# Second norms in a skewed order: the next pair's passes between a pair's root and its remainders, squares summed to a variance, remainders spread, 14 idle products for 24

## The chip, the cores and the metric

The kernel is one program on one core of one Trainium2 chip. The metric is the device time in microseconds of one execution, lower is better. Five engines run side by side, each through its own queue in order: PE (TensorE, matrix products; its weight loads are listed as PEld), DVE (VectorE), ACT (ScalarE), POOL (GpSimd), and SP (SyncE), which here only issues DMAs.

## The reference

Input is a sequence of 2048 rows of 640 channels, in fp32. Two blocks, each behind a layer norm with a modulation and a gated residual, are applied one after the other:

```python
mod = (_silu(c) @ w_mod).reshape(c.shape[0], 6, 1, -1)
sa, ca, ga, sb, cb, gb = (mod[:, 0], mod[:, 1], mod[:, 2], mod[:, 3], mod[:, 4], mod[:, 5])
h = _layernorm(x, axis=-1) * (1 + ca) + sa
x = x + ga * _A_ref(h, A_k, A_v, A_shift_k, A_ssm_k, A_ssm_D)
h = _layernorm(x, axis=-1) * (1 + cb) + sb
x = x + gb * _B_ref(h, B_w1, B_b1, B_w2, B_b2)
```

`_A_ref` is a short convolution, a product, a long convolution over the sequence and a gate. `_B_ref` is a token mixer: **a second layer norm of h**, then `u = gelu(h^T w1 + b1)` with 1728 hidden units, then `u w2 + b2`. So between block A and block B each row of x goes through two norms in a row: the first over x, with the modulation `(1 + cb)`, `sb`, and the second over its result. The change concerns that place alone.

## The kernel before

Rows and channels: the 2048 rows stand as 16 groups j of 128 rows (one row per partition), 640 channels each, in `xa` (j 0 to 7) and `xb` (j 8 to 15). Two groups make a pair; the pairs are 0 to 7.

The first 270 us or so compute block A, channel block by channel block. Its last part, `i1` and `gate` for the last channel block, finishes x. Then comes the stage of the two norms, whose results feed the first product of block B, x h against w1. The hidden units stand in 14 blocks f. The first four are accumulated side by side while the norms still run: `products(pr)` adds the two groups of a pair to the four blocks f 0 to 3, each held in a PSUM tile (`acc`). The later blocks (f from 4) take all 16 groups at a time, one block after the other, and need no more of the norms. After them come the products with w2.

fp32 accuracy is had by splitting: every operand is a rounded "half" (fp32r) and a "rest", the difference. A product is half x half, half x rest, rest x half; so one pair costs 2 groups x 4 blocks x 3 kinds x 2 column halves = 48 matmuls of 128x320.

For a pair pr the steps of the stage are:

- `x1_stats`: on DVE, the mean and variance of two groups of x (`bn_stats` for the last channel block, `bn_aggr`, lines 548 and 717).
- `root_in(n)` and `root(n)`: 1/sqrt(variance + eps). `roots` (line 721) lists which second norms and which first norms share one root, since a root is a few short instructions whose cost hardly depends on how many values it holds. Before, POOL adds eps, and turns the sum of squares into a variance (lines 737 and 740); ACT takes the square root (line 741); DVE takes the reciprocal and one Newton step (lines 326 to 329), and the first norm's shift (line 750).
- `norm1(pr)`: on ACT, (x - mean)/sigma into x itself or, for j < 4, into other memory (line 755).
- `second(pr)`: on DVE, two passes over each group: times `(1 + cb)` with a running sum (line 761), then less the mean and plus `sb` (line 766). Then on ACT the sum of squares (line 771).
- `halves(pr)`: on ACT, the row scaled by its second root, rounded (line 775). `rests(pr)`: on DVE, the difference (line 779).
- `products(pr)`: on PE (line 445).

Beside the norms, the rows of w1 for blocks 0 to 3 have to be split too: `split_rows(r, ...)` takes the fourth r of the groups, ACT makes the halves (line 420), DVE the remainders (line 422, listed under the helper's line 57). `load_rows` brings r = 2 and 3 into `x` and `p`; when `x` has been read, `load_w(4)` loads the weights of block 4 into it. After the stage `split_w(4)` splits block 4 (lines 434 and 436) and `u_evac(f, ...)` takes the first four blocks out of PSUM through gelu, freeing PSUM tiles in the order f = 0, 1, 2, 3; block 4 is accumulated in the tile that f = 0 leaves.

The order of everything is the order in which the code issues it (a manual schedule): each engine works through its own instructions in that order and waits at the head of its queue. The idle products of line 817 (results overwritten) stand on PE ahead of `products(0)`.

Of the kernel before, what the change touches and what calls it, by code (L numbers as in the profile page):

```python
# [47 lines left out]
def mixer_kernel(ctx: ExitStack, tc: tile.TileContext, q, k, v, shift_k, ssm_k, ssm_D, w1, b1, w2, b2, c,  # L48
# [7 lines left out]
    act, dve, pool, pe, sync = nc.scalar, nc.vector, nc.gpsimd, nc.tensor, nc.sync  # L56
# [3 lines left out]
    def mem(tag, n, name=None):  # L60

        return sb.tile([128, n], F32, name=name or tag, tag=tag, bufs=1)
# [261 lines left out]
    def newton(r, t, v, n=None):  # L324

        dve.reciprocal(r, t)
        dve.scalar_tensor_tensor(t, r, -0.5, r, op0=ALU.mult, op1=ALU.mult)
        TT(dve, t, t, v, ALU.mult)
        dve.scalar_tensor_tensor(r, t, 1.5, r, op0=ALU.add, op1=ALU.mult)
# [384 lines left out]
    def x1_stats(js):  # L714
        for j in js:
            x1s(NC - 1, j)()
            dve.bn_aggr(mv[:, j, :], bst[:, j])


    V_, T_, R_ = (T_kt[:, o:o + 32] for o in (1280, 1312, 1344))  # L720
    place = {}
    roots = (((), (0, 1)), ((0, 1), (2, 3)), ((2, 3), (4, 5)), ((4, 5), (6, 7, 8, 9)), ((6, 7), (10, 11)),
             ((8, 9), (12, 13)), ((10, 11), (14, 15)), ((12, 13), ()), ((14, 15), ()))
    start = []
    for second_, first_ in roots:
# [5 lines left out]

    def root_in(n):

        second_, first_ = roots[n]
        o = start[n]
        if second_:
            pool.tensor_scalar(V_[:, o:o + 2], V_[:, o:o + 2], 1 / D, EPS, op0=ALU.mult, op1=ALU.add)
            o += 2
        if first_:
            pool.tensor_scalar(V_[:, o:start[n + 1]], mv[:, first_[0]:first_[-1] + 1, 1], EPS, None, op0=ALU.add)  # L740
        act.activation(T_[:, start[n]:start[n + 1]], V_[:, start[n]:start[n + 1]], AF.Sqrt)

    def root(n):

        o = slice(start[n], start[n + 1])
        newton(R_[:, o], T_[:, o], V_[:, o])
        first_ = roots[n][1]
        if first_:
            f = slice(first_[0], first_[-1] + 1)
            dve.scalar_tensor_tensor(nm1[:, f], mv[:, f, 0], -1.0, R_[:, start[n + 1] - len(first_):start[n + 1]],  # L750
                                     op0=ALU.mult, op1=ALU.mult)

    def norm1(pr):
        for j in (2 * pr, 2 * pr + 1):
            act.activation(row(j), XR(j), AF.Identity, scale=at(R_, 1, j), bias=nm1[:, j:j + 1])

    def second(pr):

        for j in (2 * pr, 2 * pr + 1):
            t = row(j)  # L760
            dve.scalar_tensor_tensor(t, t, 1.0, CB, op0=ALU.mult, op1=ALU.mult, accum_out=su[:, j:j + 1])
        n = su[:, 2 * pr:2 * pr + 2]
        dve.tensor_scalar(n, n, msb, -1 / D, op0=ALU.add, op1=ALU.mult)
        for j in (2 * pr, 2 * pr + 1):
            t = row(j)
            dve.scalar_tensor_tensor(t, t, su[:, j:j + 1], SB, op0=ALU.add, op1=ALU.add)
        for j in (2 * pr, 2 * pr + 1):
            if j == 12:
                H.extend(unit(mem("xa", 5120, "h_x"), 4))
            H[j] = H[j][:, 0:640], H[j][:, 640:1280]  # L770
            act.activation(H[j][1].bitcast(F32R), row(j), AF.Square, accum_out=at(V_, 2, j))

    def halves(pr):
        for j in (2 * pr, 2 * pr + 1):
            act.activation(H[j][0].bitcast(F32R), row(j), AF.Identity, scale=at(R_, 2, j))

    def rests(pr):
        for j in (2 * pr, 2 * pr + 1):
            dve.scalar_tensor_tensor(H[j][1].bitcast(F32R), row(j), at(R_, 2, j), H[j][0], op0=ALU.mult,
                                     op1=ALU.subtract)  # L780
# [32 lines left out]
    for r, t in ((2, X), (3, P)):  # L813
        load_rows(r, t)
    acc.append(psum().rearrange("p (h m) -> p h m", h=2))
    for i in range(24):
        pe.matmul(acc[0][:, i % 2, 0:320], blk[0][0][:, 0].bitcast(F32R),
                  blk[1][0].rearrange("p j m -> p (j m)")[:, 0:320].bitcast(F32R), start=True, stop=True)
    second(0)
# [43 lines left out]
    products(7)  # L863

    U = {}
    thirds = lambda t, n, o=0: [t[:, o + 320 * i:o + 320 * i + 320] for i in range(n)]
# [323 lines left out]
```

## Time and profile before

| what | value |
|---|---|
| times of three runs | 675.30, 676.17, 678.89 us; median 676.17 us |
| profiled execution: first to last instruction (span) | 673.9 us |
| its mean granted TensorE clock | 0.979 |
| busy PE / DVE / ACT / POOL | 628.9 / 497.5 / 300.1 / 133.5 us |
| the same inside 268 to 356 us | 79.3 / 70.5 / 52.9 / 5.4 us |

The profiled execution has no time of its own beside its span in what is shown; the median of the runs is 2.27 us above that span, the fastest run 1.4 us. In the timeline a row is: start, length, engine, line, operation, output and inputs, shapes, count, and in brackets how long the engine had been idle and what ended that. Starts are in microseconds from the start of the span. A row's length includes the pipeline's tail, so that consecutive rows overlap a little: what an instruction costs its engine is the distance to the next start.

### The profile page before, as it was taken

The numbers are of one execution on the slowest core, as the hardware profiler recorded it, in microseconds if no ns is written. First come the engines' busy times: TensorE is split into PE (matmuls) and PEld (weight loads), VectorE is DVE, ScalarE is ACT, GpSimd is POOL, SyncE is SP. The second block draws the span as 40 slices with busy tenths as digits, with TensorE's granted clock in tenths as the row PEclk, the third lists the DMA queues.
The fourth block names the chain that finished last, engine by engine and source line by source line (L and its number), as shares of the span: only waits on it lengthen the run. The fifth ranks groups of instructions, "written<-read, shape, count | busy, mean of one in ns | idle before, by whom it ended". The sixth has DMA issues, their size and how long they took to land.

```text
span 673.9 us, 20760 instructions
## 1 busy us (share of the span) xinstructions
PE 628.9 (93%) x9119; PEld 596.1 (88%) x9119; DVE 497.5 (74%) x869; ACT 300.1 (45%) x483; POOL 133.5 (20%) x157
## 2 busy tenths in 40 slices
PE   6878887999999998999899999999999999999997
PEld 2878576989989996799789889999999999999997
DVE  7798698889798379788866621231589969888895
ACT  1564474647557465447654222322344143333331
POOL 5772068126133241000000000000000430000000
PEclk9999899999999999698999999999999999999999
DMA  9999897475426252430308333334352626356601
GB/s 185 214 266 259 277 181 160 94 147 115 67 66 217 60 154 65 107 81 1 63 3 154 63 62 65 63 63 116 98 147 71 190 77 182 115 147 168 187 32 39
DMA packets 166538, 81.23 MB, mean 121 GB/s; under 512 B 90830, under 2 KB 156912, under 8 KB 166448
## 3 DMA queue, kind: packets, MB, share of 16 engines
q1 hardware_dynamic: 159276, 78.32, 47.8%
q10 hardware_dynamic: 6916, 1.31, 1.2%
q8 instruction: 71, 1.16, 0.7%
q0 software_dynamic: 256, 0.28, 0.2%
q14 instruction: 19, 0.16, 0.1%
HBM read 69.40 MB, written 10.49 MB: 119 GB/s over the span
## 4 chain that ended last, share of the span: by engine, by line
PE 67%; DVE 16%; ACT 6%; issue 4%; DMA 3%; SPq 2%; POOL 1%; ACTq 0%; DVEq 0%; POOLq 0%
PE pst L445 20%; PE pst L1046 16%; PE pst L1123 7%; PE pst L223 7%; PE pst L271 6%; PE pst L242 6%; DVE p L57 2%; PE pst L291 2%; ACT z L280 2%; DVE tap L57 2%; PE tap L351 2%; PE pst L919 1%; DVE kt L57 1%; DMA y<-in_A_ssm_k_dram 1%; DVE aux L57 1%
## 5 line engine op out<-in xcount | busy, mean ns | idle before, releaser
L242 PE MATMUL pst<-z,w 128*64 128x64 f32 x2560 | 78.9, 223 | 13.5 <-DVE p L57 7.6
L242 PEld LDWEIGHTS pst<-z,w 128*64 128x64 f32 x2560 | 76.7, 138 | 16.3 <-issue 8.8
L57 POOL TENSOR_TENSOR y<-p 128x256 f32<-128x256 f32 x72 | 51.2, 740 | 39.7 <-DVE p L57 39.4
L229 ACT ACTIVATE z<-pst 128x1024 f32<-128x1024 f32 (+2 forms) x45 | 43.0, 974 | 35.0 <-PE pst L223 34.9
L57 DVE TENSOR_TENSOR p<-pst,kt 128x512 f32<-128x512 f32 x80 | 50.7, 680 | 8.6 <-ACT kt L246 8.6
L882 ACT ACTIVATE pst<-pst,sm 128x640 f32<-128x640 f32 x13 | 10.0, 766 | 75.8 <-PE pst L445 75.8
L271 PEld LDWEIGHTS pst<-v,y 32*128 32x128 f32 x1280 | 38.2, 187 | 6.0 <-issue 5.6
L271 PE MATMUL pst<-v,y 32*128 32x64 f32 x1280 | 40.2, 272 | 3.0 <-issue 2.9
L1046 PE MATMUL pst<-r_z,m_w 128*128 128x320 f32 x222 | 41.6, 309 | 0.1
L246 ACT ACTIVATE kt<-pst 128x512 f32<-128x512 f32 x40 | 23.9, 597 | 33.9 <-PE pst L242 17.1
L223 PE MATMUL pst<-v,p 128*64 128x128 f32 x640 | 36.7, 274 | 1.6 <-ACT p L168 1.6
L223 PEld LDWEIGHTS pst<-v,p 128*64 128x64 f32 x640 | 34.8, 137 | 3.0 <-ACT p L168 2.6
L57 POOL TENSOR_TENSOR m_p<-u_i,r_z 128x320 f32<-128x320 f32 x1 | 0.9, 870 | 183.4 <-issue 183.4
L1034 ACT ACTIVATE m_w<-m_v 128x896 fp32r<-128x896 f32 x24 | 22.7, 951 | 31.5 <-PE pst L1046 16.8
L57 DVE TENSOR_TENSOR tap<-tap,kt 128x512 f32<-128x512 f32 x51 | 35.5, 697 | 1.3
L223 PE MATMUL pst<-v,x 128*64 128x128 f32 x512 | 34.2, 291 | 2.0 <-issue 1.5
L1046 PEld LDWEIGHTS pst<-r_z,m_w 128*128 128x128 f32 x222 | 34.8, 188 | 0.4 <-DVE m_w L57 0.4
L223 PEld LDWEIGHTS pst<-v,x 128*64 128x64 f32 x512 | 30.9, 147 | 3.2 <-issue 2.5
L280 ACT ACTIVATE z<-pst 128x512 f32<-128x512 f32 x38 | 20.9, 644 | 24.0 <-PE pst L271 24.0
L57 DVE TENSOR_TENSOR m_w<-m_v,m_w 128x896 fp32r<-128x896 f32 x24 | 27.9, 1165 | 2.5 <-ACT m_w L1034 2.1
L57 DVE TENSOR_TENSOR kt<-in,tap 128x512 f32<-128x512 f32 x42 | 28.8, 686 | 1.2
L445 PE MATMUL pst<-r_z,wb0b 128*128 128x320 f32 x180 | 28.2, 310 | 0.9 <-DVE u_x L57 0.9
(308 smaller groups left out, 1497.5 us busy)
## 6 DMA issues: line engine op xcount, KB each, us to landing
x<-in_B_w_dram SPq DMA_DIRECT2D x20, 512.0 KB
m_x<-xs SPq DMA_DIRECT2D x28, 160.0 KB
out_dram<-m_x SPq DMA_DIRECT2D x28, 160.0 KB
aux<-in_A_ssm_k_dram SPq DMA_DIRECT2D x8, 512.0 KB
m_v<-in_B_w_dram SPq DMA_DIRECT2D x9, 448.0 KB
in<-in_w_mod_dram SPq DMA_DIRECT2D x4, 960.0 KB
x<-in_B_w_dram SPq DMA_DIRECT2D x7, 448.0 KB
in<-in_A_v_dram SPq DMA_DIRECT2D x22, 128.0 KB
```

Of the source, the lines that this page charges most:

```text
L57: TT = lambda eng, o, a, b, op: eng.tensor_tensor(o, a, b, op=op)
L223: pe.matmul(ps[64 * ri:64 * ri + 64, o:o + 255:2], lhs, F1[:, 128 * ri:128 * ri + 128], start=True, stop=True)
L229: act.activation(Z[:, side, t, :, k0:k1], ps.rearrange("p (a k e) -> p a k e", a=4, e=2)[:, :, k0:k1], AF.Copy)
L242: pe.matmul(ps[64 * h:64 * h + 64, o:o + 64], W2[k1 // 32][:, 2 * (k1 % 32) + ri], rhs, start=True, stop=True)
L246: act.activation(kt.rearrange("p (m i) -> p m i", i=32), pv[:, :, 1], AF.Copy)
L271: pe.matmul(pp[qd // 2][:, o:o + 64], Y[p, ri, i:i + 2].rearrange("p i k -> p (i k)"), V2[p, 64 * ri:64 * ri + 64], start=ri == 0, stop=ri ...
L280: act.activation(o, i, AF.Copy)
L291: pe.matmul(ps[64 * b:64 * b + 64, 512 * e + 64 * jj:512 * e + 64 * jj + 64], V1[p, ri, n2], T2[p, :, 32 * ri + n2], start=ri == 0, stop=r ...
L445: pe.matmul(ps[0:m, h, 0:320], w_.bitcast(F32R), r_[:, 320 * h:320 * h + 320].bitcast(F32R), start=first and i == 0, stop=last and i == 2)
L1034: act.activation(W[n][0].bitcast(F32R), A[p, w_], AF.Copy)
L1046: pe.matmul(bank[n], w[:, i].bitcast(F32R), r.bitcast(F32R), start=i == 0 and k == 0, stop=i == 6 and k == 2)
L1123: pe.matmul(acc[s][:, h, 0:320], w[:, f_].bitcast(F32R), u[r + h].bitcast(F32R), start=f_ == 0 and k == 0, stop=f_ == NF - 1 and k == 2)
```

## The change

Five edits, all in the stage of the norms.

1. **Order.** In the loop over pairs, `second(pr + 1)` now stands between `root(pr + 1)`, which yields the second root of pair pr, and `rests(pr)`. Before, `rests(pr - 1)` stood behind `second(pr)`, and the root of a pair came straight after its own `second`, statistics in between.
2. **Roots regrouped.** First norms 6 and 7 (pair 3) are now rooted together with 4 and 5 in root 2, and the statistics of groups 6 and 7 stand ahead of the second `gate`. 8 and 9 stay in root 3.
3. **No POOL step.** The squares are scaled by 1/sqrt(D), so that their sum is the variance; `bn_aggr` writes mean and variance into the same table; ACT's square root adds eps by its bias; the Newton step adds eps inside an instruction that was there. 15 small POOL instructions go.
4. **Remainders spread.** The split of the w1 rows for r = 2 and 3 goes two blocks at a time over four places, where it went four blocks at a time over two.
5. **Idle products and the end.** 14 in place of 24; and `u_evac(0)` stands ahead of `split_w(4)`.

```diff
-    roots = (((), (0, 1)), ((0, 1), (2, 3)), ((2, 3), (4, 5)), ((4, 5), (6, 7, 8, 9)), ((6, 7), (10, 11)),
+    roots = (((), (0, 1)), ((0, 1), (2, 3)), ((2, 3), (4, 5, 6, 7)), ((4, 5), (8, 9)), ((6, 7), (10, 11)),
...
     def root_in(n):
-        second_, first_ = roots[n]
-        o = start[n]
-        if second_:
-            pool.tensor_scalar(V_[:, o:o + 2], V_[:, o:o + 2], 1 / D, EPS, op0=ALU.mult, op1=ALU.add)
-            o += 2
-        if first_:
-            pool.tensor_scalar(V_[:, o:start[n + 1]], mv[:, first_[0]:first_[-1] + 1, 1], EPS, None, op0=ALU.add)
-        act.activation(T_[:, start[n]:start[n + 1]], V_[:, start[n]:start[n + 1]], AF.Sqrt)
+        o = slice(start[n], start[n + 1])
+        act.activation(T_[:, o], V_[:, o, 1], AF.Sqrt, bias=epsc)
 
     def root(n):
         o = slice(start[n], start[n + 1])
-        newton(R_[:, o], T_[:, o], V_[:, o])
+        r, t = R_[:, o], T_[:, o]
+        dve.reciprocal(r, t)
+        dve.scalar_tensor_tensor(t, r, -0.5, r, op0=ALU.mult, op1=ALU.mult)
+        dve.scalar_tensor_tensor(t, V_[:, o, 1], EPS, t, op0=ALU.add, op1=ALU.mult)
+        dve.scalar_tensor_tensor(r, t, 1.5, r, op0=ALU.add, op1=ALU.mult)
...
-            act.activation(H[j][1].bitcast(F32R), row(j), AF.Square, accum_out=at(V_, 2, j))
+            act.activation(H[j][1].bitcast(F32R), row(j), AF.Square, scale=D ** -0.5, accum_out=V_[:, place[2, j], 1:2])
...
-    for i in range(24):
+    for i in range(14):
...
     second(1)
+    x1_stats(range(6, 8))
+    split_rows(2, X, (0, 1), True, False)
     gate(NC - 1, ps, 1, dve, then=(lambda: root_in(2), lambda: root(2), lambda: halves(1), lambda: norm1(2)))
...
     second(2)
-    x1_stats(range(6, 10))
-    root_in(3)
-    root(3)
-    halves(2)
     norm1(3)
-    rests(2)
-    norm1(4)
-    products(2)
-    for pr in range(3, 8):
-        second(pr)
-        if pr > 3:
-            rests(pr - 1)
-            products(pr - 1)
-        if pr in (4, 6):
-            split_rows(pr // 2, X if pr == 4 else P, range(4), False, True)
-        if pr < 6:
-            x1_stats(range(2 * pr + 4, 2 * pr + 6))
+    x1_stats(range(8, 10))
+    for pr in range(2, 8):
         root_in(pr + 1)
         root(pr + 1)
         halves(pr)
         if pr < 6:
             norm1(pr + 2)
-        if pr in (3, 5):
-            split_rows(pr // 2 + 1, X if pr == 3 else P, range(4), True, False)
-        if pr == 4:
+        t, r, fs = X if pr < 4 else P, 2 + (pr > 3), (2, 3) if pr % 2 else (0, 1)
+        if 2 < pr < 6:
+            split_rows(r, t, fs, True, False)
+        if pr < 7:
+            second(pr + 1)
+        rests(pr)
+        products(pr)
+        if pr < 5:
+            x1_stats(range(2 * pr + 6, 2 * pr + 8))
+        if pr < 6:
+            split_rows(r, t, fs, False, True)
+        if pr == 3:
             load_w(4)
-    rests(7)
-    products(7)
...
+    u_evac(0, acc[0])
     split_w(4)
     load_w(5)
...
-    for f_ in range(4):
+    for f_ in range(1, 4):
         u_evac(f_, acc[f_])
```

Three places show what moves. The first is DVE's queue from the passes over pair 3 to the root that waits for their squares (reciprocal, 128x4), **before**. `xa` and `xb` are rows of x, `kt` holds the roots, `sm` the statistics, `r_v` the results of pair 2, `wb` the split rows of w1:

```order
L779 SCALAR_TENSOR_TENSOR r_v<-xa,kt,r_v 128x640 x2
L761 SCALAR_TENSOR_TENSOR xa,sm<-xa,kt 128x640 x2
L763 TENSOR_SCALAR sm<-sm 128x2
L766 SCALAR_TENSOR_TENSOR xa<-xa,sm,kt 128x640 x2
L548 BN_STATS sm<-xb 128x6
L717 BN_AGGR sm<-sm 128x2
L548 BN_STATS sm<-xb 128x6
L717 BN_AGGR sm<-sm 128x2
L326 RECIPROCAL kt<-kt 128x4
```

The same stretch in the **change**, on DVE:

```order
L759 SCALAR_TENSOR_TENSOR xa,sm<-xa,kt 128x640 x2
L761 TENSOR_SCALAR sm<-sm 128x2
L764 SCALAR_TENSOR_TENSOR xa<-xa,sm,kt 128x640 x2
L777 SCALAR_TENSOR_TENSOR r_v<-xa,kt,r_v 128x640 x2
L548 BN_STATS sm<-xb 128x6
L717 BN_AGGR kt<-sm 128x2
L548 BN_STATS sm<-xb 128x6
L717 BN_AGGR kt<-sm 128x2
L57 TENSOR_TENSOR wb_4083<-x,wb_4083 128x512
L57 TENSOR_TENSOR wb_4084<-x,wb_4084 128x512
L742 RECIPROCAL kt<-kt 128x4
```

The remainders of pair 2 moved from ahead of the passes to behind them, and two remainders of w1 rows now stand there too, so that more lies between the passes (line 766, now 764) and the root. The same pattern holds for the passes over pairs 3 to 7, with the statistics and w1 rows as far as there are any.

The second place is ACT's queue after the squares of pair 2 (`r_v` the results of pair 2, line 771 before, 769 now). **Before**, the square root of root 3 (line 741) follows the squares; then the halves of pair 2 and the first norms of pairs 3 and 4:

```order
L771 ACTIVATE r_v,kt<-xa 128x640 x2
L741 ACTIVATE kt<-kt 128x6
L775 ACTIVATE r_v<-xa,kt 128x640 x2
L755 ACTIVATE xa<-xa,sm,kt 128x640 x2
L755 ACTIVATE xb<-xb,sm,kt 128x640 x2
```

In the **change** the first norm of pair 3 (line 753) stands ahead of that square root (line 736):

```order
L769 ACTIVATE r_v,kt<-xa 128x640 x2
L753 ACTIVATE xa<-xa,sm,kt 128x640 x2
L736 ACTIVATE kt<-kt,sm 128x4
L773 ACTIVATE r_v<-xa,kt 128x640 x2
L753 ACTIVATE xb<-xb,sm,kt 128x640 x2
```

So two instructions of 640 columns moved ahead of the square root of root 3.

The third place is ACT's queue at the end of the stage (`wb0b` the split weights of block 4, `pst` a PSUM tile, `u_t` and `u_x` what leaves it). **Before**:

```order
L775 ACTIVATE h_x<-xb,kt 128x640 x2
L434 ACTIVATE wb0b<-x 128x1024 x2
L882 ACT_TABLE_LOAD
L882 ACTIVATE pst_4448<-pst_4448,sm 128x2x320
L892 ACTIVATE u_t<-pst_4448 128x320
L892 ACTIVATE u_x<-pst_4448 128x320
```

In the **change**:

```order
L773 ACTIVATE h_x<-xb,kt 128x640 x2
L873 ACT_TABLE_LOAD
L873 ACTIVATE pst_4447<-pst_4447,sm 128x2x320
L883 ACTIVATE u_t<-pst_4447 128x320
L883 ACTIVATE u_x<-pst_4447 128x320
L434 ACTIVATE wb0b<-x 128x1024 x2
```

The split of block 4 moved behind the table load and the evacuation of block 0; DVE's two remainders of `wb0b` moved with it.

More of the change, by code (lines that the diff above doesn't have):

```diff
@@ L716, in x1_stats @@
             x1s(NC - 1, j)()
-            dve.bn_aggr(mv[:, j, :], bst[:, j])
-    V_, T_, R_ = (T_kt[:, o:o + 32] for o in (1280, 1312, 1344))
+            dve.bn_aggr(V_[:, place[1, j], :], bst[:, j])
+    V_ = T_kt[:, 1280:1344].rearrange("p (n k) -> p n k", k=2)
+    T_, R_ = T_kt[:, 1344:1376], T_kt[:, 1376:1408]
     place = {}
-    roots = (((), (0, 1)), ((0, 1), (2, 3)), ((2, 3), (4, 5)), ((4, 5), (6, 7, 8, 9)), ((6, 7), (10, 11)),
+    roots = (((), (0, 1)), ((0, 1), (2, 3)), ((2, 3), (4, 5, 6, 7)), ((4, 5), (8, 9)), ((6, 7), (10, 11)),
              ((8, 9), (12, 13)), ((10, 11), (14, 15)), ((12, 13), ()), ((14, 15), ()))
@@ L732, in root_in @@
     def root_in(n):
-        second_, first_ = roots[n]
-        o = start[n]
-        if second_:
-            pool.tensor_scalar(V_[:, o:o + 2], V_[:, o:o + 2], 1 / D, EPS, op0=ALU.mult, op1=ALU.add)
-            o += 2
-        if first_:
-            pool.tensor_scalar(V_[:, o:start[n + 1]], mv[:, first_[0]:first_[-1] + 1, 1], EPS, None, op0=ALU.add)
-        act.activation(T_[:, start[n]:start[n + 1]], V_[:, start[n]:start[n + 1]], AF.Sqrt)
+        o = slice(start[n], start[n + 1])
+        act.activation(T_[:, o], V_[:, o, 1], AF.Sqrt, bias=epsc)
     def root(n):
         o = slice(start[n], start[n + 1])
-        newton(R_[:, o], T_[:, o], V_[:, o])
+        r, t = R_[:, o], T_[:, o]
[3 more added lines that the diff above has]
+        dve.scalar_tensor_tensor(r, t, 1.5, r, op0=ALU.add, op1=ALU.mult)
         first_ = roots[n][1]
         if first_:
-            f = slice(first_[0], first_[-1] + 1)
-            dve.scalar_tensor_tensor(nm1[:, f], mv[:, f, 0], -1.0, R_[:, start[n + 1] - len(first_):start[n + 1]],
-                                     op0=ALU.mult, op1=ALU.mult)
+            f, o = slice(first_[0], first_[-1] + 1), slice(start[n + 1] - len(first_), start[n + 1])
+            dve.scalar_tensor_tensor(nm1[:, f], V_[:, o, 0], -1.0, R_[:, o], op0=ALU.mult, op1=ALU.mult)
     def norm1(pr):
```

## The prediction

> **What bounds the kernel now.** I read first the windows by stage. Columns: window, its length, busy time of PE, PEld, DVE, ACT and POOL (with counts), granted clock, DMA share, GB/s.
>
> ```profile
> 268.00:356.00 88.00, 79.26 (x696) 74.17 (x697) 70.53 (x170) 52.92 (x96) 5.41 (x15) 0.89 0.25 55
> 356.00:540.00 184.00, 184.00 (x1260) 179.55 (x1259) 98.31 (x156) 55.61 (x89) 8.27 (x6) 1.00 0.42 98
> ```
>
> From 356 us on PE is busy without a break at clock 1.00, so whatever lets that part begin sooner is kept. From 268 to 356 no engine is full. There PE's timeline, from the idle products (L817) over the eight pairs to block f = 4 (last row):
>
> ```profile
> 281.45 6.56 PE L817 MATMUL pst<-wb,wb 128*128 128x320 f32 x24
> 287.85 9.58 PE L445 MATMUL pst<-r_z,wb 128*128 128x320 f32 x64
> ...
> 304.32 8.86 PE L445 MATMUL pst<-r_v,wb 128*128 128x320 f32 x48 [2.18 <-ACT r_v L775]
> ...
> 323.01 2.62 PE L445 MATMUL pst<-h_a,wb 128*128 128x320 f32 x16 [2.75 <-ACT h_a L775]
> ...
> 330.69 7.33 PE L445 MATMUL pst<-r_z,wb 128*128 128x320 f32 x48 [0.35 <-ACT r_z L775]
> 339.50 14.34 PE L445 MATMUL pst<-h_x,wb 128*128 128x320 f32 x96 [1.47 <-ACT h_x L775]
> 354.73 1.44 PE L445 MATMUL pst<-r_z,wb0b 128*128 128x320 f32 x8 [0.89 <-DVE u_x L57]
> ```
>
> The last two pairs, 96 matmuls, take 14.34 us: 0.149 each, 7.17 a pair. The 24 idle products take 6.40 up to 287.85: 0.267 each. The pairs' 384 matmuls would need 57.2 us at 0.149; they stand from 287.85 to 353.84. PE waits for halves four times (2.18, 2.75, 0.35, 1.47, each ended by ACT L775), once for a PSUM tile (0.89), and runs slow once. The clock, in short windows (window, length, PE busy, clock, DMA):
>
> ```profile
> 287.00:287.50 0.50, 0.50 (x4) 0.50 1.04 209
> 287.50:288.00 0.50, 0.50 (x5) 0.86 1.09 217
> ...
> 291.50:292.00 0.50, 0.50 (x6) 1.00 0.00 0
> ...
> 305.00:306.00 1.00, 1.00 (x5) 0.50 0.00 0
> ```
>
> The gate stands at half while the idle products run, until about 287.65, and falls again behind the idle 2.18.
>
> Halves wait for a root on DVE, and that for a square root on ACT. Rows of three engines around the roots 1 and 3; the last is the one square root in the trace that already takes eps as its bias (L335):
>
> ```profile
> 282.15 0.29 DVE L717 BATCH_NORM_AGGREGATE sm<-sm 128x2 f32<-128x30 f32 x1
> ...
> 302.54 0.19 DVE L326 RECIPROCAL kt<-kt 128x6 f32<-128x6 f32 x1 [0.59 <-ACT kt L741]
> ...
> 282.17 0.19 ACT L771 ACTIVATION_READ_ACCUMULATOR r_z<-t_g 128x1 f32 x1
> 282.96 0.21 ACT L741 ACTIVATE kt<-kt 128x4 f32<-128x4 f32 x1 [0.60 <-POOL kt L740]
> ...
> 282.43 0.19 POOL L737 TENSOR_SCALAR kt<-kt 128x2 f32<-128x2 f32 x1 [8.08 <-ACT r_z L771]
> ...
> L335 ACT ACTIVATE sm<-sm x1: 312/312/312, 75.9 to 75.9; 128x16 f32<-128x16 f32 x1
> ```
>
> The squares of pair 0 are summed at 282.36, yet the square root starts at 282.96: POOL lies between. DVE meanwhile has nothing to do (0.59 idle at root 3).
>
> **The change, part by part.** I move the old starts along each engine's new order, with these further rows. DVE: a pair's statistics (286.53 to 287.54), the gate, root 2, four w1 remainders (317.19 to 319.60), a root (321.26), the passes (322.21), the remainders (325.68), and what follows (327.27). ACT: the sums of squares of pairs 1 and 2, first norms of a pair, four w1 halves, one group's squares, a pair's halves.
>
> ```profile
> 286.53 0.29 DVE L548 BATCH_NORM_STATS2 sm<-xa 128x6 f32<-128x128 f32 x1
> ...
> 287.54 0.76 DVE L761 SCALAR_TENSOR_TENSOR t<-t,kt 128x640 f32<-128x640 f32 x1
> ...
> 290.95 1.22 DVE L57 TENSOR_TENSOR aux<-pst,aux 128x1024 f32<-128x1024 f32 x1
> 292.75 0.18 DVE L326 RECIPROCAL kt<-kt 128x4 f32<-128x4 f32 x1 [0.57 <-ACT kt L741]
> ...
> 317.19 2.49 DVE L57 TENSOR_TENSOR wb<-x,wb 128x512 fp32r<-128x512 f32 x4
> 319.60 0.28 DVE L548 BATCH_NORM_STATS2 sm<-xb 128x6 f32<-128x128 f32 x1
> ...
> 321.26 0.18 DVE L326 RECIPROCAL kt<-kt 128x4 f32<-128x4 f32 x1 [0.57 <-ACT kt L741]
> ...
> 322.21 0.82 DVE L761 SCALAR_TENSOR_TENSOR xb<-xb,kt 128x640 f32<-128x640 f32 x1
> ...
> 325.68 0.88 DVE L779 SCALAR_TENSOR_TENSOR h_a<-xb,kt,h_a 128x640 fp32r<-128x640 f32 x1
> ...
> 327.27 0.28 DVE L548 BATCH_NORM_STATS2 sm<-xb 128x6 f32<-128x128 f32 x1
> ...
> 291.72 0.19 ACT L771 ACTIVATION_READ_ACCUMULATOR r_v<-t 128x1 f32 x1
> ...
> 300.66 0.19 ACT L771 ACTIVATION_READ_ACCUMULATOR r_v<-xa 128x1 f32 x1
> ...
> 304.89 1.72 ACT L755 ACTIVATE xa<-xa,sm,kt 128x640 f32<-128x640 f32 x2
> ...
> 315.12 2.18 ACT L420 ACTIVATE wb<-x 128x512 fp32r<-128x512 f32 x4
> ...
> 325.21 0.72 ACT L771 ACTIVATE r_z<-xb 128x640 fp32r<-128x640 f32 x1
> ...
> 329.81 1.55 ACT L775 ACTIVATE r_z<-xb,kt 128x640 fp32r<-128x640 f32 x2 [0.90 <-DVE kt L329]
> ```
>
> *No POOL step.* The variance of group 3 is ready at 282.44; the square root can start near 282.5. Its length with a bias is not shown for four columns: 0.21 without a bias (the row at 282.96) is the lower end, 0.31 (L335, 16 columns) the upper; I take 0.30, from the row with the bias. It ends at 282.8, not 283.17: **0.37 earlier**. If ACT's wait for its own sum cost as much as POOL did, it would be 0; so 0 to 0.5. Later roots gain the same, but only where something waits for them.
>
> *Root 2.* All up to the end of the passes over pair 1 moves by that 0.37: the gate could start at 290.6. Now the statistics of pair 3 stand first (1.01), so the gate runs from 291.6 to 292.8. On ACT the squares end at 291.91 - 0.37 = 291.5; two w1 halves follow (half of 2.18: 1.1), then the square root until 292.9. These halves need the rows loaded by DMA; the DMA share is 0.00 from 291.5 at the latest, so they are there. Root 2 starts at 292.9 where it was 292.75: the gain is spent, **0.15 later**, with the work of one pair's statistics done early.
>
> *Root 3.* The squares of pair 2 end at 300.85 + 0.15 = 301.0. In ACT's queue first norms of pair 3 now stand ahead of the square root: 1.72 less some overlap, so 302.65, and the square root to 302.95. Behind it in the queue wait halves(2), norm1(4); DVE, done with statistics at about 301.1, idles until root 3 at **302.95, which is 0.4 later** than 302.54. POOL's removal doesn't help here; the order of ACT decides.
>
> *The loop.* From root 3 on a cycle of DVE is: root 0.95 (321.26 to 322.21), passes over the next pair 3.47 (to 325.68), remainders 1.59 (to 327.27), statistics 1.01, two w1 remainders 1.205 (half of 2.41): **8.23 us**. Does DVE wait in it? Behind the second pass the squares need 2 x 0.91 on ACT and the square root 0.30, while DVE has 1.59 + 1.01 + 1.205 = 3.8 of other work; the statistics, 1.2 ahead of the next root, come last, and 0.30 + 0.1 for the square root fits in the 1.2 of w1 remainders. So the old idle before each root is filled, with 0.8 to spare. Root 4 is then at 311.2, root 5 at 319.4, root 6 at 302.95 + 3 x 8.23 = 327.64. From a reciprocal to PE's first matmul took 1.75 (321.26 to 323.01), so pair 5 starts on PE at **329.4**, before 330.69.
>
> *Is PE late?* The 14 idle products end at 281.45 + 14 x 0.267 = 285.2; halves(0) reach PE at 282.8 + 1.75 = 284.6. At half clock until 287.65 nine matmuls run, the other 27 of blocks 0 to 2 end at 291.7; block 3 needs the tile of the gate, 292.9, and ends at 294.7; pair 1 at 301.9. Pair 2 at 302.95 + 1.75 = 304.7: idle 2.8, so I assume the gate falls as before, half clock for one 3.4 us stretch, 1.5 us lost; 313.4. Pair 3 ends at 320.5; pair 4 waits for 319.4 + 1.75 = 321.15 and ends at 328.3. PE then waits 1.1 for pair 5. So **fewer idle products and an early start of PE buy nothing**: what they gain is lost in front of pair 2. Cover is 1.1 at pair 5; if a second slow stretch took it, the end would move by 0.4.
>
> *The end.* PE from 329.4: pair 5 ends at 336.55. Root 7 has no statistics ahead, 327.64 + 7.22 = 334.86, and its halves reach PE at 336.6. Three pairs: 329.4 + 0.05 + 3 x 7.17 = **350.95**, 2.9 before 353.84.
>
> ```profile
> 348.59 2.01 ACT L434 ACTIVATE wb0b<-x 128x1024 fp32r<-128x1024 f32 x2 [2.21 <-PE pst L445]
> 350.62 1.28 ACT L882 ACT_TABLE_LOAD   x1
> 351.91 0.77 ACT L882 ACTIVATE pst<-pst,sm 128x640 f32<-128x640 f32 x1
> ...
> 349.68 2.36 DVE L57 TENSOR_TENSOR wb0b<-x,wb0b 128x1024 fp32r<-128x1024 f32 x2 [2.31 <-ACT wb0b L434]
> ...
> 354.18 0.49 DVE L57 TENSOR_TENSOR u_x<-pst,u_x 128x320 fp32r<-128x320 f32 x1 [0.50 <-ACT u_x L892]
> ```
>
> Before, the split of block 4 went first and block f = 4 waited for the tile of f = 0 until 354.67. Now the table load (1.28) runs while PE works, gelu starts when f = 0 is complete, 350.95 - 3 x 1.79 = 345.6 (12 matmuls a block), and the tile is free 2.76 later (351.91 to 354.67), at 348.4. The split's halves run 347.8 to 349.8, its remainders 348.9 to 351.2, the first half until 350.1, ahead of 350.95. So f = 4 starts at 350.95 without the 0.89: **354.73 - 350.95 = 3.78 us** in all. The load of the next weights, behind the remainders of the split, starts 0.85 earlier (352.04 to 351.2), not 3.8; it has the time of one block, 14 us, to land and be split, so PE shouldn't see it.
>
> Span 673.9 - 3.78 = 670.1. The shown span lies 2.27 under the median of the runs; I take the same distance after: 676.17 - 3.78 = **672.4 us**.
>
> **Rivals.**
>
> *The roots still wait (0.15).* Each square root now stands behind first norms and w1 halves in ACT's own queue, and waits for the sum just written. If that eats the 0.8 to spare and the usual 0.6 returns at roots 4 to 7, 4 x 0.6 = 2.4 are lost: gain 1.4, **674.8**. Against it: ACT's work in a cycle is 1.55 + 1.72 + half of 2.18 + 2 x (0.72 + 0.19) + 0.30 = 6.5 us of 8.23.
>
> *The tail stays (0.15).* If the split of block 4 comes later than 350.95, since ACT now evacuates first, PE waits about the 0.89 as before: gain 2.9, **673.3**. What decides is whether the remainders' first half is done; I have 0.85 of margin.
>
> *Slower: the gate stays at half (0.05).* 14 idle products end 2.5 us before the gate opened. Should products(0), which come with short waits, not count as dense work, the matmuls go on at 0.267. A matmul loses 0.118, so each us at half clock loses 0.44 of a full-speed us. From 285.2 the pairs need 57.2 at full speed and would end at 342.4; to end later than 354.73 the half clock must last (354.73 - 342.4)/0.44 = 28 us, until 313; until 321 it costs 0.5% more than before (**679.6**). For it: all 24 idle products ran at half. Against it: products(0) have 36 matmuls ready at 285.2, no gap before 287.65, and pair 2 got the gate open again within 3.4 us of steady matmuls.
>
> [...]
>
> **How the numbers follow.** The forecast has 0.65. Differences within 0.5% (3.4 us) can't be told from no change by a measurement of this kernel. My gain lies only 0.4 above that, and root 3 alone is uncertain by 0.3; I let 0.10 of the 0.65 fall short. Faster 0.55; within 0.5%: 0.10 + 0.15 + 0.15 = 0.40; slower 0.05. The range takes in the rivals at 674.8 and 673.3, the three runs' spread of some us in the median, and below the shorter square root and no fall of the clock: 670.5 to 675.5.
>
> **What would show it.** Right: root 3's reciprocal near 303 with DVE idle about 1.8 ahead of it; no idle before the roots 4 to 7; reciprocals 8.2 apart; PE waiting near 302 to 304.7, then under 1.2 at any pair; f = 4 near 351 with no wait. Wrong: DVE rows of 0.5 idle ended by ACT's square root in the loop; clock 0.50 beyond 288; f = 4 ended by DVE or ACT.

## The result and the profile after

| | before | after |
|---|---|---|
| median, with the range of 12 runs each | 678.19 us (675.16 to 681.10) | 672.53 us (671.15 to 677.06) |
| ratio after to before, 95% interval | | 0.9919 (0.9897 to 0.9941) |
| profiled execution: span | 673.9 us | 670.2 us |
| stage: first pass over pair 0 on DVE to first matmul of block f = 4 on PE | 277.80 to 354.73: 76.93 us | 278.70 to 350.81: 72.11 us |

The changed kernel is faster by 0.81% (0.59% to 1.03%), the forecast was 672.4 us. Single executions of one kernel differ by several microseconds (the table's ranges), so all that follows is read from the **length of the stage** in the table's last row. It is 4.82 us shorter, 0.71% of 678 us.

The windows by stage, in the columns of before (the stage ends earlier, so the first window does too):

```profile
268.00:352.00 84.00, 73.84 (x746) 70.08 (x743) 71.50 (x172) 54.64 (x98) 0.00 (x0) 0.96 0.24 52
352.00:536.00 184.00, 184.00 (x1259) 179.55 (x1259) 98.23 (x156) 55.60 (x89) 8.26 (x6) 1.00 0.44 101
```

From 352 on PE is busy without a break, as it was from 356. What the stage gained is kept. POOL has nothing to do in it.

PE's timeline of the changed kernel, from the idle products (L815) over the eight pairs to block f = 4:

```profile
279.92 2.32 PE L815 MATMUL pst<-wb,wb 128*128 128x320 f32 x14
285.46 7.09 PE L445 MATMUL pst<-r_z,wb 128*128 128x320 f32 x36 [3.22 <-ACT r_z L773]
293.68 4.38 PE L445 MATMUL pst<-r_z,wb 128*128 128x320 f32 x28 [1.13 <-DVE aux L57]
...
305.24 8.87 PE L445 MATMUL pst<-r_v,wb 128*128 128x320 f32 x48 [2.48 <-ACT r_v L773]
313.95 7.23 PE L445 MATMUL pst<-h_a,wb 128*128 128x320 f32 x48
321.42 2.61 PE L445 MATMUL pst<-h_a,wb 128*128 128x320 f32 x16 [0.24 <-ACT h_a L773]
...
329.50 7.32 PE L445 MATMUL pst<-r_z,wb 128*128 128x320 f32 x48 [0.76 <-ACT r_z L773]
336.66 14.31 PE L445 MATMUL pst<-h_x,wb 128*128 128x320 f32 x96
350.81 2.80 PE L445 MATMUL pst<-r_z,wb0b 128*128 128x320 f32 x18
```

Two large waits for halves stand early (3.22 ahead of pair 0, 2.48 ahead of pair 2; the 1.13 between them is for a PSUM tile), then 0.24 and 0.76, and none ahead of pair 6 and block 4, where before had 1.47 and 0.89. Pair 2 takes 8.87 against 7.32 for pair 5: it ran at half clock for a while (the last section has the clock).

The roots on DVE (root 1, root 3, root 4 with what stands before it, root 5, then roots 6 and 7), and ACT around root 3:

```profile
283.77 0.18 DVE L742 RECIPROCAL kt<-kt 128x4 f32<-128x4 f32 x1 [0.42 <-ACT kt L736]
...
303.56 0.18 DVE L742 RECIPROCAL kt<-kt 128x4 f32<-128x4 f32 x1 [1.70 <-ACT kt L736]
...
310.51 1.22 DVE L57 TENSOR_TENSOR wb<-x,wb 128x512 fp32r<-128x512 f32 x2
311.65 0.17 DVE L742 RECIPROCAL kt<-kt 128x4 f32<-128x4 f32 x1
...
312.52 0.83 DVE L759 SCALAR_TENSOR_TENSOR xb<-xb,kt 128x640 f32<-128x640 f32 x1
...
316.00 1.67 DVE L777 SCALAR_TENSOR_TENSOR h_a<-xa,kt,h_a 128x640 fp32r<-128x640 f32 x2
...
319.74 0.17 DVE L742 RECIPROCAL kt<-kt 128x4 f32<-128x4 f32 x1
...
327.82 0.17 DVE L742 RECIPROCAL kt<-kt 128x4 f32<-128x4 f32 x1
...
334.96 0.16 DVE L742 RECIPROCAL kt<-kt 128x2 f32<-128x2 f32 x1
...
301.62 1.72 ACT L753 ACTIVATE xa<-xa,sm,kt 128x640 f32<-128x640 f32 x2
303.24 0.28 ACT L736 ACTIVATE kt<-kt,sm 128x4 f32<-128x4 f32 x1
```

At root 3 DVE idles 1.70, since ACT does the first norms of pair 3 (301.62) ahead of the square root (303.24). Roots 4 to 7 have no bracket: no idle time. Roots 4 and 5 stand 8.09 apart.

### The profile page after: what moved, and what is told of

The parts are those of the page before. It is cut to its first block, busy times and chain, and to the rows that moved or that the text cites. A ratio compares the mean times of both kernels' runs of the same rounds, so it can differ in the third digit from the quotient of the medians.

```text
span 670.2 us, 20718 instructions
## 1 busy us (share of the span) xinstructions
PE 622.5 (93%) x9109; PEld 591.4 (88%) x9109; DVE 496.5 (74%) x869; ACT 300.5 (45%) x483; POOL 128.0 (19%) x142
## 3 DMA queue, kind: packets, MB, share of 16 engines
q8 instruction: 71, 1.16, 0.7%
## 4 chain that ended last, share of the span: by engine, by line
PE 68%; DVE 17%; ACT 4%; issue 4%; DMA 4%; SPq 2%; POOL 0%; ACTq 0%; DVEq 0%; POOLq 0%
PE pst L445 22%; PE pst L1038 16%; PE pst L1115 7%; PE pst L223 7%; PE pst L271 6%; PE pst L242 5%; DVE p L57 3%; PE pst L291 2%; DVE tap L57 2%; ACT z L280 2%; PE pst L910 1%; PE tap L351 1%; DMA y<-in_A_ssm_k_dram 1%; DVE aux L57 1%; DVE sm L548 1%
## 5 line engine op out<-in xcount | busy, mean ns | idle before, releaser
L445 PE MATMUL pst<-r_z,wb 128*128 128x320 f32 x144 | 24.0, 326 | 5.1 <-ACT r_z L773 4.0
```

Source lines behind the costliest of these rows:

```text
L445: pe.matmul(ps[0:m, h, 0:320], w_.bitcast(F32R), r_[:, 320 * h:320 * h + 320].bitcast(F32R), start=first and i == 0, stop=last and i == 2)
```

## The experiments

Each run's stage, from the first pass over `t_g` on DVE to the first matmul with `wb0b` on PE:

| kernel | stage, us | against after |
|---|---|---|
| before | 277.80 to 354.73: 76.93 | +4.82 |
| after | 278.70 to 350.81: 72.11 | |
| after, taken again | 276.61 to 348.73: 72.12 | +0.01 |
| split of block 4 first again | 280.06 to 353.23: 73.17 | +1.06 |
| 24 idle products | 283.14 to 355.26: 72.12 | +0.01 |
| no idle products | 281.33 to 353.44: 72.11 | 0.00 |
| first norms of pair 3 earlier | 278.85 to 349.71: 70.86 | -1.25 |
| POOL's step back | 277.11 to 350.30: 73.19 | +1.08 |
| before, without POOL's step | 279.72 to 354.21: 74.49 | +2.38 |
| remainders not spread | 278.08 to 351.35: 73.27 | +1.16 |
| remainders on POOL, first norms earlier | 277.28 to 350.36: 73.08 | +0.97 |
| first norms earlier, late remainders | 278.62 to 348.77: 70.15 | -1.96 |

The changed kernel gives 72.11 and 72.12 in two executions, whose spans are 670.2 and 668.1, so differences of some tenths of a microsecond mean something here, which they don't in the time of one execution (the single times of the runs below that were not repeated lie between 670.89 and 676.46 us, and not in the order of their stages).

### The changed kernel again

> The changed kernel itself, timed once more beside the variant with late remainders on the same chip. Theory: the stage is 72.1 again, whether the clock falls ahead of pair 2 or not; the median lies 0.6% to 1.0% under the kernel before. [...]

Stage 72.12; median 673.48 us of 12 runs, beside 677.98 us of 17 runs of before, ratio 0.9943 (0.9917 to 0.9969). The two intervals overlap, and the 0.71% of the stage lies in both. By the ratio the gain is 0.57%, just short of the 0.6% expected as the least. Pair 2 took 8.82 here, so the clock fell again; the case without a fall comes with 24 idle products below.

### The end: the split of block 4 ahead of the evacuation again

```diff
-    u_evac(0, acc[0])
     split_w(4)
...
-    for f_ in range(1, 4):
+    for f_ in range(4):
```

> The changed kernel with one piece put back: the split of block 4 again ahead of the evacuation of block f = 0. I read the length of the stage, from the first pass over pair 0 on DVE to the first matmul of block f = 4 on PE: 76.93 us before, 72.11 after. Theory (the new order at the end is worth the wait that it removed, 0.89): 73.0, with a wait of 0.8 to 1.0 in front of block 4 ended by DVE's u_x. Rival (the products now end so that the old order would do as well): 72.1 and no wait.

PE's rows for the last two pairs and block 4:

```profile
338.04 14.31 PE L445 MATMUL pst<-h_x,wb 128*128 128x320 f32 x96
353.23 2.91 PE L445 MATMUL pst<-r_z,wb0b 128*128 128x320 f32 x18 [0.89 <-DVE u_x L57]
```

The wait of before is back, 0.89 by DVE's u_x; the stage is 73.17. The theory holds, and its price is 1.06 rather than 0.89: the products' length in a row, 14.31, includes a tail that overlaps the next matmul when there is no wait. In the changed kernel the next one starts 350.81 - 336.66 = 14.15 after them, here 15.19.

### The number of idle products

```diff
-    for i in range(14):
+    for i in range(24):
```

> The changed kernel with 24 idle products, as before, in place of 14. Theory (their number buys nothing, since the products of pairs 0 and 1 are held up by the gate's tile and pair 2 waits for its halves anyway): the stage stays at 72.1 +- 0.2, pair 2 still begins on PE 1.7 behind its reciprocal. Rival (they delay pair 0 and 1, 10 x 0.15 to 0.27 = 1.5 to 2.7 us, and the delay is kept): 73.5 to 74.8.

And the loop left out altogether:

> The changed kernel without any idle products (their results are overwritten, so nothing that is computed changes). Theory (they buy nothing): the stage is 72.1 +- 0.2; the products of pairs 0 and 1 run at half clock for longer, but end before pair 2's halves come. Rival (without them the gate opens late enough that pair 2 starts late): 72.5 to 74.

Pair 2 on PE, with 24 idle products and then with none:

```profile
309.67 7.32 PE L445 MATMUL pst<-r_v,wb 128*128 128x320 f32 x48 [2.47 <-ACT r_v L773]
```

```profile
307.87 8.87 PE L445 MATMUL pst<-r_v,wb 128*128 128x320 f32 x48 [2.48 <-ACT r_v L773]
```

72.12 and 72.11: the number of idle products buys nothing, between 0 and 24. The two rows show something else that I had no right to expect. Behind the same idle time, 2.47 and 2.48, pair 2 ran at full clock in one execution and lost 1.5 in the other. The stage has the same length, so this loss costs nothing either: pair 4 starts when its halves come.

### Root 3: the first norms of pair 3 ahead of the passes over pair 2

```diff
+    norm1(3)
     second(2)
-    norm1(3)
     x1_stats(range(8, 10))
```

> The changed kernel with one move: the first norms of pair 3 on ACT stand ahead of the passes and squares of pair 2, where ACT had 2.4 us without work, and no longer between those squares and the square root of root 3. Theory (that place in ACT's queue sets root 3, and everything behind hangs on it): DVE's idle time at root 3 falls from 1.70 to about 0.4, root 3 and all later roots come 1.3 earlier, the stage is 70.8. Rival (PE, not the roots, sets the end, or the gate's fall moves too): root 3 earlier, the stage still 71.8 to 72.3.

Root 3 on DVE, pair 2 and block 4 on PE:

```profile
302.44 0.18 DVE L742 RECIPROCAL kt<-kt 128x4 f32<-128x4 f32 x1 [0.42 <-ACT kt L736]
...
304.13 7.33 PE L445 MATMUL pst<-r_v,wb 128*128 128x320 f32 x48 [1.20 <-ACT r_v L773]
...
349.71 2.80 PE L445 MATMUL pst<-r_z,wb0b 128*128 128x320 f32 x18
```

The idle time at root 3 falls from 1.70 to 0.42. Counted from the stage's start, root 3 comes 1.27 earlier, and the stage is 1.25 shorter. So ACT's order at root 3 set everything behind it, and the change had given away 1.25 us there. What is left of the wait is ended by the square root (302.11, 0.30 long), which waits for the last statistics on DVE.

### POOL's step put back into the changed order

```diff
-        act.activation(T_[:, o], V_[:, o, 1], AF.Sqrt, bias=epsc)
+        k = len(roots[n][0])
+        if k:
+            p = slice(start[n], start[n] + k)
+            pool.tensor_scalar(V_[:, p, 1], V_[:, p, 1], 1.0, EPS, op0=ALU.mult, op1=ALU.add)
+        if roots[n][1]:
+            p = slice(start[n] + k, start[n + 1])
+            pool.tensor_scalar(V_[:, p, 1], V_[:, p, 1], EPS, None, op0=ALU.add)
+        act.activation(T_[:, o], V_[:, o, 1], AF.Sqrt)
...
-        dve.scalar_tensor_tensor(t, V_[:, o, 1], EPS, t, op0=ALU.add, op1=ALU.mult)
+        TT(dve, t, t, V_[:, o, 1], ALU.mult)
```

> The changed kernel with POOL's step put back between squares and square root (eps added on POOL, the square root without a bias, the Newton step as before); order, spreading, scaling and the end stay as changed. Theory (the order fills DVE's time with other work, so the step is hidden at roots 4 to 7 and shows only at roots 1 and 3, 0.4 each): the stage is 72.1 to 73.1, most likely 72.9, without idle time at roots 4 to 7. Rival (the step's removal is what gained the time, 0.57 to 0.6 at each of the roots 1 to 7): 74 or more, with idle rows of about 0.5 at roots 4 to 7.

The roots 1, 4 and 7 on DVE, and pair 6 on PE:

```profile
282.52 0.18 DVE L749 RECIPROCAL kt<-kt 128x4 f32<-128x4 f32 x1 [0.76 <-ACT kt L743]
...
310.44 0.17 DVE L749 RECIPROCAL kt<-kt 128x4 f32<-128x4 f32 x1
...
334.38 0.17 DVE L749 RECIPROCAL kt<-kt 128x2 f32<-128x2 f32 x1 [0.32 <-ACT kt L743]
...
336.12 14.34 PE L445 MATMUL pst<-h_x,wb 128*128 128x320 f32 x96 [0.29 <-ACT h_x L780]
```

73.19, 0.09 beyond the range of the theory and 0.8 under the rival. Root 1 waits 0.76 instead of 0.42. Roots 4 to 6 don't wait, as the theory had it. What it had missed is root 7, which has no statistics of another pair ahead of it: there the step shows again (0.32), and pair 6 on PE waits 0.29 where it had no wait. Nor does the step show at root 3, where the theory had 0.4: DVE idles 1.61 there, beside 1.70 without the step, for the first norms on ACT hide it.

The 1.08 is not POOL's step alone, since the Newton step went back to its old form too. Up to root 3 the stage loses 0.30. From root 3 to root 6, where no more is waited than before, it loses 0.23: the next instruction of the Newton step starts 0.27 after the last one (310.64 to 310.91) where it took 0.20 (311.85 to 312.05 in the changed kernel), and a root costs 0.08 more. From root 6 to root 7 it loses 0.48, behind root 7 the last 0.07.

### POOL's step taken out of the kernel before

Only the third edit of the change, on the old order.

> The kernel before with one part of the change alone: no POOL step (squares scaled to the variance, eps by the bias of the square root and inside the Newton step); the old order stays. Stage length: 76.93 before, 72.11 with all edits. Theory (in the old order each root waits for its own squares, so the step counted at each of the roots 1 to 7 from which the end hangs; part of it is taken by PE's own work): the stage is 74.9, between 74.0 and 75.5. Rival (the order carries the whole gain, and the old order has another bound behind the step): 76.5 to 76.9.

Roots 4 and 5 on DVE, and the pairs 4 and 6 and block 4 on PE:

```profile
311.63 0.18 DVE L742 RECIPROCAL kt<-kt 128x4 f32<-128x4 f32 x1 [0.42 <-ACT kt L736]
...
321.51 0.18 DVE L742 RECIPROCAL kt<-kt 128x4 f32<-128x4 f32 x1 [0.42 <-ACT kt L736]
...
323.19 2.62 PE L445 MATMUL pst<-h_a,wb 128*128 128x320 f32 x16 [2.55 <-ACT h_a L773]
...
338.99 14.33 PE L445 MATMUL pst<-h_x,wb 128*128 128x320 f32 x96 [1.00 <-ACT h_x L773]
354.21 2.91 PE L445 MATMUL pst<-r_z,wb0b 128*128 128x320 f32 x18 [0.90 <-DVE u_x L57]
```

74.49: inside the theory's range, so the old order pays for the step at most of its roots. 2.44 of the 4.82 come by this edit alone (the new form of the Newton step is part of it). Roots 4 and 5 still wait 0.42, the two stand 9.88 apart (four w1 remainders lie between them), and the wait ahead of block 4 is 0.90.

### The remainders not spread

```diff
-        if pr < 6:
-            split_rows(r, t, fs, False, True)
+        if pr in (3, 5):
+            split_rows(r, t, range(4), False, True)
```

> The changed kernel with the w1 remainders not spread: four at a time behind the passes over pairs 4 and 6, none behind those over pairs 3 and 5. Theory (the remainders also hide the square root; where none stands ahead of a root, DVE waits 0.4): idle rows of 0.42 at roots 4 and 6 and none at 5 and 7; root 7 comes 0.84 later, since both waits and all remainders lie ahead of it, pair 6 starts 0.8 later on PE, the stage is 72.9. Rival (their place doesn't matter, as the sum of DVE's work is the same): 72.1, without idle rows.

Roots 4 to 7 on DVE and pair 6 on PE:

```profile
310.40 0.18 DVE L742 RECIPROCAL kt<-kt 128x4 f32<-128x4 f32 x1 [0.42 <-ACT kt L736]
...
319.70 0.17 DVE L742 RECIPROCAL kt<-kt 128x4 f32<-128x4 f32 x1
...
327.16 0.18 DVE L742 RECIPROCAL kt<-kt 128x4 f32<-128x4 f32 x1 [0.42 <-ACT kt L736]
...
335.52 0.16 DVE L742 RECIPROCAL kt<-kt 128x2 f32<-128x2 f32 x1
...
337.18 14.34 PE L445 MATMUL pst<-h_x,wb 128*128 128x320 f32 x96 [1.00 <-ACT h_x L773]
```

The idle rows stand exactly where no remainder is left, at roots 4 and 6. The stage is 73.27, by 0.4 more than expected, so the rival falls: their place does matter. Root 7 comes 32.58 behind root 3 (302.94), where it came 31.40 behind it in the changed kernel: 1.18, not 0.84; beside the two waits of 0.42 each of the four cycles took some 0.08 more than the sum that I had made.

### The remainders on POOL

The four pieces of w1 remainders in the loop on POOL instead of DVE, with the first norms of pair 3 moved as above.

> The changed kernel with the first norms of pair 3 ahead of the passes over pair 2, and with the four spread pieces of w1 remainders in the loop given to POOL, which has nothing else to do there. Theory (DVE's cycle of 8.09 sets the pace of roots 4 to 6; without the remainders it is 6.95, so that PE with 7.2 a pair becomes the bound): the stage is 68 to 69.5, and the waits in front of pairs 4 to 6 are gone. Rival (POOL is slow at 128x512 subtractions or takes them at DVE's cost, so that DVE's passes get longer by what was moved): 70.5 to 73.

POOL's first and last pair of subtractions, and the DVE instructions beside them (a Newton step of root 2, root 6, a Newton step of root 7):

```profile
291.58 2.52 POOL L57 TENSOR_TENSOR wb<-x,wb 128x512 fp32r<-128x512 f32 x2 [33.62 <-ACT wb L420]
292.91 1.21 DVE L744 SCALAR_TENSOR_TENSOR kt<-kt 128x6 f32<-128x6 f32 x1
...
326.63 0.18 DVE L742 RECIPROCAL kt<-kt 128x4 f32<-128x4 f32 x1 [0.43 <-ACT kt L736]
...
331.21 3.65 POOL L57 TENSOR_TENSOR wb<-p,wb 128x512 fp32r<-128x512 f32 x2 [4.86 <-ACT wb L420]
333.81 1.06 DVE L743 SCALAR_TENSOR_TENSOR kt<-kt 128x2 f32<-128x2 f32 x1
```

73.08: the theory is out, and the stage lies just past the rival's range, 2.22 above the run with the same move of the first norms alone. Two subtractions of 128x512 take about 3.65 us on POOL in the loop (2.52 for the first two, ahead of it) and 1.14 on DVE. The Newton step on 128x6, 0.17 in the run with the first norms alone, took 1.21; it ended at 294.12, POOL's work at 294.10. The one of root 7, 0.16 otherwise, took 1.06 and ended at 334.87, POOL's at 334.86. Root 2 was 1.27 longer for that, and from root 7 to its halves it took 0.90 longer. In between, in the second and the third cycle, a rest beside POOL took 1.93 where it takes 0.88, so that of the 1.14 saved in a cycle 1.05 went again, and with no remainder ahead of the roots 4 to 6 each waits 0.42 for its square root (326.63): from root 3 to root 6 it took 0.2 longer than with the remainders on DVE.

### Late remainders

With the first norms moved, one w1 remainder goes ahead of root 3, into its 0.42 of idle time; those of row quarter 3 go one cycle later; pair 6's products take the two last blocks' remainders at their end.

```diff
     x1_stats(range(8, 10))
+    split_rows(2, X, (0,), False, True)
+    lows = {2: (2, X, (1,)), 3: (2, X, (2, 3)), 5: (3, P, (0, 1)), 6: (3, P, (2, 3))}
```

> The changed kernel with three moves. The first norms of pair 3 stand ahead of the passes over pair 2, as in the run with that move alone (stage 70.86). One of the four w1 remainders of the first cycle moves ahead of root 3, into 0.42 of idle time. The two of row quarter 3 that stood ahead of root 6 go behind it, and the last two of that quarter behind root 7 (the products of pair 6 take those two last). Theory (DVE's work up to root 6 sets the end, what can wait past root 6 comes off the path, until PE itself, 7.17 a pair, is the bound): root 6 comes 0.42 + 1.14 earlier than in that run, PE's waits ahead of pairs 4 and 5 shrink to under 0.4, the stage is 69.7 (69.4 to 70.1); time by the median 0.3% to 0.4% below the changed kernel. Rival (what is put off is needed again at once: PE waits as long for the remainders at pair 6 or 7, or DVE's root 7 and 8 get late): 70.6 to 71.2.

Roots 3, 5 and 6 on DVE; pair 4, pair 7 (from its third matmul on) and block 4 on PE:

```profile
302.23 0.16 DVE L742 RECIPROCAL kt<-kt 128x4 f32<-128x4 f32 x1
...
317.80 0.17 DVE L742 RECIPROCAL kt<-kt 128x4 f32<-128x4 f32 x1
325.25 0.18 DVE L742 RECIPROCAL kt<-kt 128x4 f32<-128x4 f32 x1 [0.42 <-ACT kt L736]
...
319.47 2.61 PE L445 MATMUL pst<-h_a,wb 128*128 128x320 f32 x16 [0.76 <-ACT h_a L773]
...
341.91 7.02 PE L445 MATMUL pst<-h_x,wb 128*128 128x320 f32 x46 [0.26 <-DVE h_x L777]
348.77 2.80 PE L445 MATMUL pst<-r_z,wb0b 128*128 128x320 f32 x18
```

The stage is 70.15, just above the theory's range and 0.71 under the run with the first norms alone, where I had expected 1.16. Pair 5's wait is nearly gone (between 326.75 and 327.00 PE is busy for 0.11 of 0.25 us); pair 4 still waits 0.76. By taking both remainders from ahead of root 6 I took its cover too, and the idle row of 0.42 is there (325.25). But pair 6 begins 1.23 earlier than in the run with the first norms alone (55.48 against 56.71 from the stage's start); what is lost is lost behind it. The last two pairs take 14.67 up to block 4, not 14.15, with a new wait of 0.26 for pair 7's rests. On DVE these stand behind root 8, and that behind the remainders that were put off. Whether root 6's lost cover alone makes this wait was not tried. Median 670.35 us of 6 runs, ratio to before 0.9902 (0.9872 to 0.9933). Beside the changed kernel's 673.48 on the same chip that is 0.46% less; its interval and that of the changed kernel overlap, and the stage, 1.96 shorter (0.29%), is what carries the claim that it is the fastest of the three.

## Why the prediction was right

The forecast case, faster by more than 0.5%, came true. In the two profiled executions the stage began 0.90 later after the change, though ahead of it only root 0 had changed; so I compare times from the stage's start.

| step, us from the stage's start | predicted | after |
|---|---|---|
| root 1 (reciprocal) | 282.82 - 277.80 = 5.02 | 5.07 |
| root 2 | 15.10 | 14.97 |
| root 3 | 25.15 | 24.86 |
| root 6 | 49.84 | 49.12 |
| pair 5 on PE | 51.60 | 50.80 |
| pair 6 on PE | 58.82 | 57.96 |
| block f = 4 on PE | 73.15 | 72.11 |

Every step of the table came in the order and by the mechanism predicted, and the end 1.04 sooner. The terms that were mis-sized:

- **Root 2 and root 3**, 0.13 and 0.16: the square root of root 2 was done when the gate ended, where I had it 0.1 later; at root 3 the first norms overlap the rows on both sides a little more than I let them (301.62 to 303.24, 1.62 and not 1.65, and they start before the squares' row has ended).
- **The cycle**, 3 x 0.14 = 0.43: 8.09, not 8.23. The root takes 0.87 (311.65 to 312.52), not 0.95, and the two remainders 1.14 (310.51 to 311.65), not 1.205. The shorter root is the new form of the Newton step, which the prediction put at nothing; the passes (3.48 to 316.00), rests and statistics are as predicted.
- **From the reciprocal to PE**, 1.68 rather than 1.75, and at pair 6 no wait of 0.05.
- **The last two pairs**, 0.19: I added the length of the row, 14.34, where the distance to the next start, 14.15, is what PE needs.

The other claims, one by one:

- *No wait at roots 4 to 7, 0.8 to spare*: right. The first square root in the loop ends at 310.99 and root 4 starts at 311.65, so 0.66 were to spare. What covers it are the w1 remainders: without them the wait is back (three runs).
- *POOL's removal shows only where something waits*: right in the new order, where it is worth 1.08 with the Newton step by the run that puts both back, against 2.44 in the old order. My list of places was short by roots 7 and 8.
- *Root 3 is set by ACT's order, and given away*: right; moving that one pair of instructions gains 1.25.
- *Idle products buy nothing; a fall of the clock ahead of pair 2 costs nothing*: right, by runs with 0, 14 and 24, with and without the fall. The forecast that the clock falls was luck: pair 2 lost time by it in five of the twelve executions (8.82 to 8.87 us, against 7.32 or 7.33 in the other seven). So was the early part: I had the idle products at half clock until 285.2 and no gap behind them, but in the profiled execution 14 took 2.32, PE idled 3.22 ahead of pair 0 and its first 36 matmuls took 7.09; in the execution taken again the 14 took 4.10 and there was no gap. The stage is the same.
- *The end*: right. Block 0's tile was free at 348.48 and the first half of the split's remainders at about 350.1, ahead of 350.81. So the rival in which the end still waits is out, and its mechanism has a price, 1.06, from the run that restores it.
- The rival in which the roots wait is out by the rows of roots 4 to 8; the slower one, the gate at half to beyond 313, by the clock: full again from 308.12 before and from 310.12 after, and pair 3 took 7.23 to 7.33 in every execution.

How the 4.82 are made up can't be read from the pieces put back singly (POOL's step 1.08, the unspread remainders 1.16, the end 1.06) and the piece taken alone (POOL's step 2.44): the parts cover for each other. A chain of these kernels can be added up, stretch by stretch, by the starts of the rows (us):

| stretch | before | before, without POOL's step | remainders not spread | after | first norms earlier |
|---|---|---|---|---|---|
| stage's start to root 3 | 24.74 | 23.63 | 24.86 | 24.86 | 23.59 |
| root 3 to root 7 | 35.22 | 33.97 | 32.58 | 31.40 | 31.42 |
| root 7 to pair 6 on PE | 1.74 | 1.67 | 1.66 | 1.70 | 1.70 |
| pair 6 to block f = 4 on PE | 15.23 | 15.22 | 14.17 | 14.15 | 14.15 |

From root 3 to root 7 DVE has the same passes, rests, statistics and eight w1 remainders in all five. There the new order (with the regrouped roots) saves 1.39 and the spreading 1.18. But up to root 3 the change loses 1.23, so that of the new order only 0.16 is left until the first norms move. The end gives 1.05. Along another chain the shares would be others. What the new place of the rests gives alone, without the regrouped roots, was not tried.

The runs gave 0.81% and 0.57%, the forecast was 0.56%, the stage 0.71%. That the median came out so near 672.4 is partly chance: the gain was 1.04 larger than predicted, but the median of before in these runs, 678.19 us, was also 2.02 above the one from which I had started, and the span to time distance was 1.8 instead of 2.27.

## What to carry to other kernels

A short chain across engines (squares, square root, reciprocal) is hidden by putting other work of the waiting engine between its start and its end; that cover is then part of the schedule, and whoever moves it gets the wait back, as three runs here did. When an instruction on another engine sets such a chain, look at what stands ahead of it in that engine's own queue: here two instructions in the wrong place cost 1.25 us, a quarter of what the whole change gained. And sum distances between starts, not lengths of rows.

## What was not expected of the hardware

**The clock and 2.5 us of idle time.** Ahead of pair 2 PE idles 2.47 or 2.48 us in the changed kernel and its near variants. In the changed kernel's execution the clock then fell (window, length, PE, PEld, DVE, ACT and POOL busy, granted clock, DMA share, GB/s):

```profile
306.00:306.50 0.50, 0.50 (x5) 0.50 (x4) 0.43 (x4) 0.50 (x1) 0.00 (x0) 1.00 0.00 0
306.50:307.00 0.50, 0.50 (x5) 0.50 (x4) 0.50 (x1) 0.50 (x2) 0.00 (x0) 0.71 0.00 0
307.00:307.50 0.50, 0.50 (x4) 0.50 (x3) 0.50 (x2) 0.50 (x2) 0.00 (x0) 0.50 0.00 0
```

It fell some 1.5 us after the matmuls had started again, and pair 2 took 8.87. The execution taken again (2.47, 8.82) and those without idle products and with unspread remainders (2.48 and 2.47, 8.87 and 8.86) are like it; those with the split put back and with 24 idle products idled 2.48 and 2.47 and ran through at 7.33 and 7.32. So the same idle time came with a fall in four of these six executions and without one in two. Nor does its length sort the others: in the kernel before, pair 2 took 8.86 behind 2.18, while it ran through at 7.32 behind 2.43 with POOL's step back, and at 7.33 behind 2.21 in the kernel before without POOL's step. Behind the 1.20 to 1.25 of the three runs with the first norms earlier it took 7.33 each time. What decided is not shown.

In the traces of before and after the clock's changes lie whole steps apart. Before, it was at half from 267.16 to 273.98, from 277.40 to 287.64 and from 304.70 to 308.12, after from 286.23 to 289.64 and from 306.71 to 310.12 (read in windows of 0.1 us). So it stayed at half for 3.41, 6.83 or 10.24 us and was full between for 3.41 or 17.07: one, two, three and five times 3.41. The first of the two falls after came 0.77 us behind the start of pair 0, ahead of which PE had idled 3.22.

**POOL beside DVE.** In the run with remainders on POOL the two Newton steps of 1.21 and 1.06 us ended within 0.02 of POOL's work, and a rest beside POOL took 1.93 instead of 0.88, 1.05 more. Other DVE instructions beside POOL took no longer than elsewhere: statistics 0.28 and 0.24 (from 316.61 and 317.13, POOL busy from 314.23 to 317.83), the reciprocal of root 7 0.15 (from 333.63, POOL busy from 331.21 to 334.86). POOL was slower too: two subtractions took 2.52 in the first piece and 3.60 to 3.66 in the later ones, beside rests. What made these instructions longer is not shown. The price here was 1.05 us of DVE in a cycle, for 1.14 that it was spared.
